# Decode attention on one core: score matmuls of four kv heads on the four 32-column groups of the PE array

## The chip, the cores and the metric

The kernel runs on one core of a Trainium2 chip. The metric is device time in microseconds; the numbers are medians of two to seven runs, which lie within about 1% of their median. A run more than 1.5% above the fastest of its kernel is called slow; the medians quoted include them, ratios and clock ranges leave them out. The profile is one execution taken by the hardware profiler; its span, from the first to the last instruction, is about 2 us shorter than the time. PE is the TensorE, PEld its weight loads, DVE the VectorE, ACT the ScalarE, POOL the GpSimd, SP the engine whose queue issues all loads here. "Granted clock" is the share of full speed that the throttle granted to the TensorE. SBUF and PSUM are on-chip memories: the loads fill SBUF, the TensorE's results land in PSUM, and to evict is to copy them from there to SBUF. A column group is 32 neighbouring columns of the TensorE's array of 128; a tile is the part of the array that one matmul uses.

## The reference

One decode step of grouped-query attention over the last 512 positions of a cache. There are 32 batches, 32 query heads, 8 kv heads, head size 128 and model size 512, all in bf16.

```python
q = (x @ wq)                                  # [32, 1, 512] @ [512, 4096] -> 32 heads of 128
k = repeat(k_cache[:, :, 2048 - 512:, :], 4)  # 8 kv heads, each for 4 query heads
v = repeat(v_cache[:, :, 2048 - 512:, :], 4)
scores = einsum("bhqd,bhkd->bhqk", q, k) * 128 ** -0.5
o = einsum("bhqk,bhkd->bhqd", softmax(scores), v)
return o.reshape(32, 1, 4096) @ wo            # [4096, 512]
```

K and V of one batch are 1 MB each, 64 MB in all; wq and wo are 4 MB each. (These MB are of 2^20 bytes; all loads together are 75.5 million bytes, and the profile counts in millions.)

## The kernel before

For each batch `b` the TensorE transposes K (32 matmuls against an identity), DVE and ACT evict K^T from PSUM to SBUF (six and two pieces of 512 columns), and eight score matmuls follow, one for each kv head. Four batches (a "quad") share one PSUM tile of 128 rows, 32 rows for each batch. Softmax, the transposes of P and the V matmuls are done a quad at a time.

```python
def load_k(b):                                  # on the SP queue; load_v is alike, with 12 buffers
    if b >= NK:                                 # NK = 4
        sp.wait_ge(pe_T3, b - NK + 1)           # buffer free: transposes of batch b - 4 done
    sp.dma_start(K_sb[:, b % NK, :, :],         # runs of KT * DH = 512 elements, 1 KB
        k_cache[b, :, SK - W:, :].rearrange("g (p kt) d -> p g (kt d)", kt=KT)).then_inc(sem_k[b % NK], 16)
# order of the loads: K0, wq, V0, K1, V1, ... K31, V31, wo

def s_matmuls(b):
    ...                                         # waits for Q of this batch and for a free PSUM tile
    for g in range(G):                          # 8 kv heads
        ...                                     # waits for the eviction of K^T of head g
        last = pe.matmul(
            S_ps[32 * j:32 * (j + 1), q % 2, :],        # j = b % 4
            lhsT=QBD[:, b % NQB, g, :],                 # 32 columns, 4 of them not zero
            rhs=KT_sb[:, b % NKT, g, :],
            start=(g == 0), stop=(g == G - 1), tile_position=(0, 32 * j))
```

All eight score matmuls of one batch use the same 32 columns of the array, so they run one after the other.

## Time and profile before

| | before |
|---|---|
| median (range), 3 runs | 229.98 us (229.43 to 230.52) |
| span of the profile | 228.2 us |
| TensorE busy | 77% |
| bytes moved by the load queue | 75.6 MB |
| mean granted clock | 0.882 |

These are lines of the page of the kernel before: the busy times of the engines, then, in 40 slices of 5.7 us, the busy share of the 16 DMA engines in tenths (9 is 90% or more), and the GB/s that they moved.

```profile
PE 176.6 (77%) x2501; PEld 124.7 (55%) x2501; DVE 90.0 (39%) x237; ACT 48.1 (21%) x93; POOL 9.4 (4%) x43
...
DMA  6999999999999999999999999999999999999950
GB/s 188 386 385 348 348 348 349 348 348 350 349 347 348 349 347 348 348 348 348 348 348 348 347 348 348 348 348 348 347 347 348 347 348 347 349 345 329 350 183 6
```

DMA is at 9 from the second slice to the 38th, and the rate is 348 GB/s in nearly all of them. It is higher, 385 and 386 GB/s, in the two slices in which wq is loaded. The rows below are of the same page's list of groups: engine, operation, output and inputs, count, then busy time in us and mean ns of one instruction, then the idle time before them and what ended most of it.

```profile
L234 PE MATMUL KT_ps<-ident,K_sb 128*128 128x128 bf16 x1024 | 74.3, 240 | 29.7 <-DMA K_sb<-in_k_cache_dram 25.6
...
L254 PE MATMUL S_ps<-KT_sb,QBD 128*32 128x512 bf16 x256 | 68.2, 414 | 2.8 <-POOL QBD L191 2.8
```

The transposes (L234) and the score matmuls (L254) are the two large items on PE. The next lines are from the list of waits (total us, times, longest): transposes that wait for K to land, and score weight loads that wait for an eviction.

```profile
PE KT_ps L234 <- DMA K_sb<-in_k_cache_dram: 25.6, 16, 2.3
...
PEld S_ps L254 <- DVE KT_sb L348: 5.9, 26, 0.3
```

The list of waits of the load queue itself names the wait for K buffers:

```profile
SPq L132 <- PE KT_ps L234: 39.8, 19, 3.5
```

One batch in the timeline (start us, duration us): the six DVE evictions, the eight score matmuls, the two ACT evictions.

```profile
141.27 2.08 DVE L348 COPY KT_sb<-KT_ps 128x512 bf16<-128x512 bf16 x6 [3.77 <-PE KT_ps L234]
...
142.44 1.90 PE L254 MATMUL S_ps<-KT_sb,QBD 128*32 128x512 bf16 x8
142.60 1.08 ACT L405 ACTIVATE KT_sb<-KT_ps 128x512 bf16<-128x512 bf16 x2 [4.77 <-PE KT_ps L234]
```

And the end of the kernel, from the same view: the first projection matmuls start at 219.61, the last eight wait 0.58 us for the last piece of wo, and the store is issued at 226.30.

```profile
219.61 3.93 PE L315 MATMUL KT_ps<-wo_sb,oT_sb 128*32 128x512 bf16 x32 [0.80 <-DVE oT_sb L370]
...
222.50 0.14 PEld L315 LDWEIGHTS KT_ps<-wo_sb,oT_sb 128*32 128x32 bf16 x8 [0.58 <-DMA wo_sb<-in_wo_dram]
...
226.30 0.35 SPq L162 DMA_DIRECT2D out_dram<-out_sb  x1
```

### The profile page before, as it was taken

Reading aid. Unit: us, or ns where it says so; the run is one execution under the profiler, and the core shown is the slowest. Engines: PE = TensorE matmul, PEld = TensorE weight load, DVE = VectorE, ACT = ScalarE, POOL = GpSimd, SP = SyncE. Lnnn points to the kernel's source line nnn. Section 1 sums busy time; section 2 is a strip of 40 time slices with the busy share of each in tenths; the row PEclk is TensorE's granted clock in tenths of the full one; section 3 lists DMA queues with packets and bytes.
Section 4 is the critical chain, followed back from the end, with each engine's and each line's share of the span. In section 5 each row is a group of like instructions: output and inputs, shape, how many; then the busy total and the mean of one; then the engine's idle time right before and its main releaser. Section 6 shows DMA issues by size and latency. Waiting matters only on the chain.

```text
span 228.2 us, 5628 instructions
## 1 busy us (share of the span) xinstructions
PE 176.6 (77%) x2501; PEld 124.7 (55%) x2501; DVE 90.0 (39%) x237; ACT 48.1 (21%) x93; POOL 9.4 (4%) x43
## 2 busy tenths in 40 slices
PE   0184968669869986995997996699669799999482
PEld 0182555447635753575564964477437656695340
DVE  0047333351535243633275243524353317644212
ACT  2000103122113211320133021321132013403203
POOL 5002000000000000000000000000000000000000
PEclk9998879999997999797699889889997859979855
DMA  6999999999999999999999999999999999999950
GB/s 188 386 385 348 348 348 349 348 348 350 349 347 348 349 347 348 348 348 348 348 348 348 347 348 348 348 348 348 347 347 348 347 348 347 349 345 329 350 183 6
DMA packets 72950, 75.90 MB, mean 333 GB/s; under 512 B 1184, under 2 KB 70880, under 8 KB 72928
## 3 DMA queue, kind: packets, MB, share of 16 engines
q1 hardware_dynamic: 72928, 75.57, 103.7%
q8 instruction: 19, 0.31, 0.6%
q14 instruction: 3, 0.02, 0.0%
HBM read 75.53 MB, written 0.03 MB: 331 GB/s over the span
## 4 chain that ended last, share of the span: by engine, by line
DMA 53%; PE 26%; SPq 16%; issue 2%; DVEq 0%; DVE 0%; ACT 0%
DMA K_sb<-in_k_cache_dram 48%; PE KT_ps L234 12%; PE S_ps L254 7%; PE QO_ps L286 6%; SPq L142 6%; DMA wo_sb<-in_wo_dram 5%; SPq L132 5%; SPq L149 4%; SPq L124 2%; PE PT_ps L266 1%; PE KT_ps L315 0%; DVEq L43 0%; DVE X_sb L389 0%; PE QO_ps L324 0%; ACT out_sb L441 0%
## 5 line engine op out<-in xcount | busy, mean ns | idle before, releaser
L234 PE MATMUL KT_ps<-ident,K_sb 128*128 128x128 bf16 x1024 | 74.3, 240 | 29.7 <-DMA K_sb<-in_k_cache_dram 25.6
L348 DVE COPY KT_sb<-KT_ps 128x512 bf16<-128x512 bf16 x192 | 68.0, 418 | 68.0 <-PE KT_ps L234 67.3
L234 PEld LDWEIGHTS KT_ps<-ident,K_sb 128*128 128x128 bf16 x1024 | 67.8, 108 | 42.1 <-DMA K_sb<-in_k_cache_dram 34.9
L254 PE MATMUL S_ps<-KT_sb,QBD 128*32 128x512 bf16 x256 | 68.2, 414 | 2.8 <-POOL QBD L191 2.8
L405 ACT ACTIVATE KT_sb<-KT_ps 128x512 bf16<-128x512 bf16 x64 | 34.7, 594 | 161.6 <-PE KT_ps L234 161.6
L254 PEld LDWEIGHTS S_ps<-KT_sb,QBD 128*32 128x32 bf16 x256 | 23.7, 102 | 34.8 <-issue 8.2
L286 PEld LDWEIGHTS QO_ps<-PT_sb,V_sb 128*128 128x128 bf16 x768 | 20.0, 97 | 3.2 <-ACT PT_sb L422 2.1
L286 PE MATMUL QO_ps<-PT_sb,V_sb 128*128 128x4 bf16 x768 | 20.7, 165 | 0.8 <-ACT PT_sb L422 0.7
L370 DVE CAST oT_sb<-QO_ps 128x128 bf16<-128x128 f32 x8 | 5.8, 719 | 38.8 <-PE QO_ps L286 38.8
L191 POOL COPY QBD<-QT_sb 128x32 bf16<-128x32 bf16 x32 | 6.3, 209 | 152.7 <-PE S_ps L254 135.8
L214 PE MATMUL QO_ps<-xT_sb,big_sb 128*128 128x32 bf16 x128 | 4.1, 185 | 8.4 <-DMA big_sb<-in_wq_dram 8.3
L336 DVE CAST QT_sb<-QO_ps 128x512 bf16<-128x512 f32 x2 | 4.8, 2393 | 13.0 <-PE QO_ps L214 13.0
L214 PEld LDWEIGHTS QO_ps<-xT_sb,big_sb 128*128 128x128 bf16 x128 | 3.8, 103 | 8.7 <-issue 6.7
L286 PEld LDWEIGHTS QO_ps<-PT_sb,big_sb 128*128 128x128 bf16 x256 | 6.5, 96 | 0.8 <-ACT PT_sb L422 0.8
L286 PE MATMUL QO_ps<-PT_sb,big_sb 128*128 128x4 bf16 x256 | 6.7, 164 | 0.0
L413 ACT ACTIVATE P_f_56<-S_ps,negmax 128x512 f32<-128x512 f32 x8 | 5.5, 687 | 4.0 <-DVE negmax L356 4.0
L354 DVE TENSOR_REDUCE maxv<-S_ps 128x1 f32<-128x512 f32 x8 | 5.5, 682 | 1.0 <-PE S_ps L254 1.0
L266 PE MATMUL PT_ps<-ident,P_bf 128*128 128x128 bf16 x32 | 3.6, 242 | 2.5 <-DVE P_bf L364 2.5
L422 ACT ACTIVATE PT_sb<-PT_ps 128x512 bf16<-128x512 bf16 x8 | 4.8, 604 | 1.2 <-PE PT_ps L266 1.2
L315 PE MATMUL KT_ps<-wo_sb,oT_sb 128*32 128x512 bf16 x32 | 3.9, 626 | 0.9 <-DVE oT_sb L370 0.8
L266 PEld LDWEIGHTS PT_ps<-ident,P_bf 128*128 128x128 bf16 x32 | 2.5, 111 | 3.0 <-DVE P_bf L364 3.0
L364 DVE TENSOR_SCALAR P_bf<-P_f_56,recip 128x512 bf16<-128x512 f32 x8 | 3.9, 486 | 0.3
(25 smaller groups left out, 14.7 us busy)
## 6 DMA issues: line engine op xcount, KB each, us to landing
K_sb<-in_k_cache_dram SPq DMA_DIRECT2D x32, 1024.0 KB, 12.1
V_sb<-in_v_cache_dram SPq DMA_DIRECT2D x24, 1024.0 KB, 12.0
big_sb<-in_v_cache_dram SPq DMA_DIRECT2D x8, 1024.0 KB, 12.0
big_sb<-in_wq_dram SPq DMA_DIRECT2D x4, 1024.0 KB, 10.8
wo_sb<-in_wo_dram SPq DMA_DIRECT2D x4, 1024.0 KB, 12.0
x_sb<-in_x_dram SPq DMA_DIRECT2D x1, 32.0 KB, 1.6
out_dram<-out_sb SPq DMA_DIRECT2D x1, 32.0 KB, 1.5
```

Source lines behind the costliest of these rows:

```text
L132: sp.dma_start(K_sb[:, b % NK, :, :], k_cache[b, :, SK - W:, :].rearrange("g (p kt) d -> p g (kt d)", kt=KT),).then_inc(sem_k[b % NK], 16)
L142: sp.dma_start(v_slot(b)[:, :, :], v_cache[b, :, SK - W:, :].rearrange("g (p kt) d -> p g (kt d)", kt=KT),).then_inc(sem_v[b % NV], 16)
L149: sp.dma_start(wo_sb[:, c * 8:(c + 1) * 8, :], wo[c * 1024:(c + 1) * 1024, :].rearrange("(h d) n -> d h n", d=P),).then_inc(sem_wo[c], 16)
L191: pool.tensor_copy(dst, src).then_inc(pool_qbd, 1)
L214: last = pe.matmul(QO_ps[:, hl * 32:(hl + 1) * 32], lhsT=wq_sb[:, kt, h * DH:(h + 1) * DH], rhs=xT_sb[:, kt, :], start=(kt == 0), stop=(kt ...
L234: last = pe.matmul(KT_ps[:, t, half * 512 + kt * 128: half * 512 + (kt + 1) * 128], lhsT=K_sb[:, b % NK, g, kt * DH:(kt + 1) * DH], rhs=id ...
L254: last = pe.matmul(S_ps[32 * j:32 * (j + 1), q % 2, :], lhsT=QBD[:, b % NQB, g, :], rhs=KT_sb[:, b % NKT, g, :], start=(g == 0), stop=(g = ...
L266: last = pe.matmul(PT_ps[:, kt * 128:(kt + 1) * 128], lhsT=P_bf[:, qq % 2, kt * 128:(kt + 1) * 128], rhs=ident[:, :], start=True, stop=Tru ...
L286: last = pe.matmul(QO_ps[:, j * 32 + 4 * g: j * 32 + 4 * g + 4], lhsT=v_slot(b)[:, g, kt * DH:(kt + 1) * DH], rhs=PT_sb[:, qq % 2, kt * 12 ...
L348: dve.tensor_copy(KT_sb[:, b % NKT, g, :], KT_ps[:, t, half * 512:(half + 1) * 512]).then_inc(dve_T, 1)
L370: dve.tensor_copy(oT_sb[:, :, 4 * qq:4 * qq + 4].rearrange("p h j -> p j h"), QO_ps[:, 0:128].rearrange("p (j h) -> p j h", h=HQ),).then_i ...
L405: act.activation(KT_sb[:, b % NKT, g, :], KT_ps[:, t, half * 512:(half + 1) * 512], ACTF.Copy).then_inc(act_T, 1)
```

## The change

The change puts head `g` on column group `g % 4`, so that matmuls which follow each other lie on different column groups and can overlap. Batches no longer own a column group; each accumulates into 4 rows of every group, and zeros in the weights keep the other rows unharmed. The weights, the number of matmuls and the loads stay as they are.

```diff
+        def prow(g, j):
+            return 32 * (g % 4) + 16 * (g // 4) + 4 * j
 ...    # the GpSimd copy of Q into QBD: same 32 elements a partition, other columns
                     last = pe.matmul(
-                        S_ps[32 * j:32 * (j + 1), q % 2, :],
+                        S_ps[32 * (g % 4):32 * (g % 4) + 32, q % 2, :],
                         lhsT=QBD[:, b % NQB, g, :],
                         rhs=KT_sb[:, b % NKT, g, :],
-                        start=(g == 0), stop=(g == G - 1), tile_position=(0, 32 * j),
+                        start=(j == 0 and g < 4), stop=(j == 3 and g >= 4), tile_position=(0, 32 * (g % 4)),
                     )
 ...    # the V matmuls read P^T at the new rows
-   rhs=PT_sb[:, qq % 2, kt * 128 + j * 32 + 4 * g: kt * 128 + j * 32 + 4 * g + 4],
+   rhs=PT_sb[:, qq % 2, kt * 128 + prow(g, j): kt * 128 + prow(g, j) + 4],
```

## The prediction

> **What bounds the kernel.** DMA. In 3 us windows the 16 DMA engines are fully busy (share 1.03 to 1.12) from 3 to 219 us, at 346 to 351 GB/s nearly everywhere (376 to 389 GB/s around the wq load, before 18 us; 333 to 339 GB/s from 201 to 210 us). The core must read 75.5 MB; at 348 GB/s that is 217 us of a 228.2 us span. The rest is the start and the tail after wo's last piece lands at 222.45 us (chain of waits): eight projection matmuls, PSUM copies, a summing matmul, a copy and the store. The TensorE is no limit: 176.6 us busy (77%), and its transposes wait 25.6 us for K to land (list of waits). The chain names PE for 26%, but those pieces gate the issue of loads that then queue: a K load lands 12.1 us after issue, at about 3 us of bandwidth each, so about four are outstanding.
>
> **What the change does.** Same 256 score matmuls, weight loads, bytes and pool copies; only the column group changes, so that neighbouring heads can overlap. Before, the eight matmuls of one batch used one column group and took about 1.90 us (timeline near 142 us). The Trainium skill, "TensorE: Matmul & The Clock Gate", Part 3 (measured speedup), gives 2.38x for three column tiles with 512 columns; not yet shown here. If all operands were ready, 1.90 us could fall to about 0.8 us. They are not: the six DVE evictions of K^T come 0.35 us apart (141.27 to 143.35) and the two of ACT end at 143.68, while the transposes end at 142.5. "TensorEngine Tiling (Array Packing)", PSUM Bottleneck, says that the PSUM copy may become the bottleneck after such a speedup; here the last matmul can't start before 143.7 and needs 0.38 us more, so it ends near 144.1 instead of 144.34. I estimate 0.2 to 0.4 us a batch, 6 to 12 us of PE time in all.
>
> **How much is critical.** Almost none. The freed PE time becomes waiting for K. At the end the chain from the last K to the projection may finish 0.3 us earlier, but the projection already waits 0.58 us for wo's last piece (list of waits), which lands when the bytes are through.
>
> **Predicted time:** 229.8 us, range 228.8 to 230.8 (before: 229.43 to 230.52). Chances: faster by over 2% 0.02, within 2% 0.96, slower 0.02.
>
> **What the profile would show if right.** DMA share full from 3 to 219 us, near 348 GB/s; wo's last piece lands within 1 us of 222.5; same tail. The score line's PE busy time falls from 68.2 us to 45 to 60 us; PE total from 176.6 to 160 to 172 us; the transposes' wait for K grows by several us. The score line's weight loads wait more for the DVE and ACT evictions. Mean granted clock between 0.82 and 0.90.
>
> **What would make it wrong.** (1) If 348 GB/s is not the ceiling of these loads but is held down by K buffers coming free late (the queue waits 39.8 us for PE), a faster PE would raise GB/s by up to a few per cent. (2) Column groups that follow each other could serialise; then the score line would not shrink, still hidden under DMA unless a batch needs over 6 us of PE time. (3) A lower clock in the tail, where it is already 0.5, could put the projection behind wo: about 0.5 us.

## The result and the profile after

| | before | after |
|---|---|---|
| median (range) | 229.83 us (229.43 to 230.52, 4 runs) | 229.61 us (229.38 to 229.70, 4 runs) |
| ratio, 95% interval | | 0.9994 (0.9972 to 1.0017) |

The time is the same. A ratio here and below is the mean time of one kernel's fast runs over that of the other's fast runs of the same rounds, so it is not quite the ratio of the medians that are quoted.

The lines of the page after that answer to those shown of before, engines and slices first:

```profile
PE 171.3 (75%) x2501; PEld 123.8 (54%) x2501; DVE 91.4 (40%) x237; ACT 48.0 (21%) x93; POOL 9.4 (4%) x43
...
DMA  5999999999999999999999999999999999999960
GB/s 175 387 386 350 348 348 349 348 348 349 349 348 350 348 350 351 348 348 350 348 350 348 350 349 348 350 348 349 349 348 348 349 348 349 349 339 334 347 208 6
```

Then the transposes and the score matmuls in its list of groups:

```profile
L242 PE MATMUL KT_ps<-ident,K_sb 128*128 128x128 bf16 x1024 | 83.5, 256 | 30.7 <-DMA K_sb<-in_k_cache_dram 27.2
...
L262 PE MATMUL S_ps<-KT_sb,QBD 128*32 128x512 bf16 x256 | 53.2, 449 | 3.6 <-POOL QBD L199 2.8
```

The loads look as before. The score matmuls fell from 68.2 to 53.2 us of busy time, 15.0 us less. TensorE as a whole fell only from 176.6 to 171.3 us, because the transposes, which the change doesn't touch, rose from 74.3 to 83.5 us. The mean granted clock of this run is 0.821, the lowest of the four (up to 0.870). Now the list of waits after:

```profile
PE KT_ps L242 <- DMA K_sb<-in_k_cache_dram: 27.2, 16, 3.7
...
PEld S_ps L262 <- ACT KT_sb L413: 16.7, 43, 0.7
...
PEld S_ps L262 <- DVE KT_sb L356: 12.4, 54, 0.2
```

The score matmuls now wait for the evictions of K^T: 16.7 us of idle weight loads for ACT and 12.4 us for DVE, against 5.9 us for DVE before. In the timeline, first the scores after of a batch with the evictions in step, then those of one whose first six heads were already evicted when the scores began, because its transposes had run slowly; the last line is the same batch in the kernel before, where all six were ready too:

```profile
142.15 1.69 PE L262 MATMUL S_ps<-KT_sb,QBD 128*32 128x512 bf16 x8
...
149.91 1.47 PE L262 MATMUL S_ps<-KT_sb,QBD 128*32 128x512 bf16 x8
...
150.25 1.90 PE L254 MATMUL S_ps<-KT_sb,QBD 128*32 128x512 bf16 x8
```

The view of the kernel after, cut short at 150.4 us so that only the first six matmuls of that second batch are merged into the line:

```profile
149.91 0.61 PE L262 MATMUL S_ps<-KT_sb,QBD 128*32 128x512 bf16 x6
```

The six ready matmuls took 0.61 us together. Before, eight in a row took 1.90 us. One lasts 0.38 us alone, so each further one then added about 0.22 us, and six would have taken about 1.5 us (worked out from these two). Column groups do overlap, for these six by about 2.4 times: by the kept trace four start within 0.01 us of each other, one on each group, and the other two follow 0.22 us later. The Trainium skill gives 2.38 times for three column tiles with 512 columns ("TensorE: Matmul & The Clock Gate", Part 3, Measured speedup); the trace agrees that tiles overlap, but six matmuls on four tiles are another arrangement, and that the two figures are so close is chance. The prediction's 0.8 us for eight ready matmuls is an estimate from that page's figure. But such a batch is the exception (7 of 32 stages took 1.47 us): in the usual one the matmuls come at the pace of the evictions, and the stage shrinks only from 1.90 to 1.69 us.

The next lines show a stretch of equal work in both traces, in windows of 3 us (busy us of PE, PEld, DVE, ACT, POOL, each with its count, then granted clock, DMA share and GB/s), before:

```profile
153.00:156.00 3.00, 3.00 (x111) 3.00 (x108) 0.53 (x1) 0.00 (x0) 0.00 (x0) 1.00 1.10 347
156.00:159.00 3.00, 3.00 (x31) 1.76 (x28) 2.10 (x7) 1.08 (x2) 0.00 (x0) 1.00 1.10 348
```

and after:

```profile
153.00:156.00 3.00, 3.00 (x86) 3.00 (x83) 0.78 (x2) 0.00 (x0) 0.00 (x0) 0.50 1.10 348
156.00:159.00 3.00, 3.00 (x29) 2.29 (x26) 2.21 (x6) 0.51 (x2) 0.00 (x0) 0.50 1.10 350
```

In this stretch the V matmuls and the next transposes ran at half clock, where they had run at full clock before. Over the whole traces, 376 transposes after and 206 before started about 0.107 us behind the one before them, and most others 0.056 us: 170 times 0.05 us is 8.5 us of the 9.2 us by which the transposes rose. The loads moved 347 to 350 GB/s in both. At the end of the kernel after:

```profile
218.98 3.92 PE L323 MATMUL KT_ps<-wo_sb,oT_sb 128*32 128x512 bf16 x32 [0.81 <-DVE oT_sb L378]
...
221.85 0.14 PEld L323 LDWEIGHTS KT_ps<-wo_sb,oT_sb 128*32 128x32 bf16 x8 [0.82 <-DMA wo_sb<-in_wo_dram]
...
225.66 0.35 SPq L165 DMA_DIRECT2D out_dram<-out_sb  x1
```

Everything is 0.63 to 0.65 us earlier than before, the wait for wo is 0.82 us, and the tail from there is as long as it was (store issued 3.8 us after that wait in both). This is within what runs of one kernel differ by.

### The profile page after: what moved, and what is told of

Its sections match the earlier page's. It is cut to its first block, busy times and chain, and to the rows that moved or that the text cites. A ratio compares the mean times of both kernels' runs of the same rounds, so it can differ in the third digit from the quotient of the medians.

```text
span 227.5 us, 5628 instructions
## 1 busy us (share of the span) xinstructions
PE 171.3 (75%) x2501; PEld 123.8 (54%) x2501; DVE 91.4 (40%) x237; ACT 48.0 (21%) x93; POOL 9.4 (4%) x43
## 4 chain that ended last, share of the span: by engine, by line
DMA 59%; PE 19%; SPq 16%; issue 3%; ACT 2%; DVEq 0%; DVE 0%; ACTq 0%
DMA K_sb<-in_k_cache_dram 54%; PE KT_ps L242 12%; PE QO_ps L294 6%; SPq L145 6%; DMA wo_sb<-in_wo_dram 5%; SPq L135 4%; SPq L152 4%; SPq L127 2%; ACT KT_sb L413 1%; ACT PT_sb L430 1%; PE KT_ps L323 0%; DVEq L43 0%; DVE X_sb L397 0%; PE QO_ps L332 0%; ACT out_sb L449 0%
## 5 line engine op out<-in xcount | busy, mean ns | idle before, releaser
L242 PE MATMUL KT_ps<-ident,K_sb 128*128 128x128 bf16 x1024 | 83.5, 256 | 30.7 <-DMA K_sb<-in_k_cache_dram 27.2
L242 PEld LDWEIGHTS KT_ps<-ident,K_sb 128*128 128x128 bf16 x1024 | 76.7, 118 | 38.9 <-DMA K_sb<-in_k_cache_dram 33.3
L356 DVE COPY KT_sb<-KT_ps 128x512 bf16<-128x512 bf16 x192 | 68.8, 418 | 64.3 <-PE KT_ps L242 63.1
L262 PE MATMUL S_ps<-KT_sb,QBD 128*32 128x512 bf16 x256 | 53.2, 449 | 3.6 <-POOL QBD L199 2.8
L262 PEld LDWEIGHTS S_ps<-KT_sb,QBD 128*32 128x32 bf16 x256 | 13.8, 95 | 36.5 <-ACT KT_sb L413 16.7
L421 ACT ACTIVATE P_f<-S_ps,negmax 128x512 f32<-128x512 f32 x8 | 5.5, 688 | 3.8 <-DVE negmax L364 3.8
L274 PE MATMUL PT_ps<-ident,P_bf 128*128 128x128 bf16 x32 | 3.1, 220 | 2.5 <-DVE P_bf L372 2.5
L368 DVE RECIPROCAL recip<-sums 128x1 f32<-128x1 f32 x8 | 1.3, 164 | 7.4 <-ACT P_f L421 7.4
L372 DVE TENSOR_SCALAR P_bf<-P_f,recip 128x512 bf16<-128x512 f32 x8 | 3.9, 486 | 0.3
```

The source lines that it names most:

```text
L242: last = pe.matmul(KT_ps[:, t, half * 512 + kt * 128: half * 512 + (kt + 1) * 128], lhsT=K_sb[:, b % NK, g, kt * DH:(kt + 1) * DH], rhs=id ...
L262: last = pe.matmul(S_ps[32 * (g % 4):32 * (g % 4) + 32, q % 2, :], lhsT=QBD[:, b % NQB, g, :], rhs=KT_sb[:, b % NKT, g, :], start=(j == 0 ...
L356: dve.tensor_copy(KT_sb[:, b % NKT, g, :], KT_ps[:, t, half * 512:(half + 1) * 512]).then_inc(dve_T, 1)
```

## The experiments

Theory A: the loads set the time; the score stage is beside the critical path, and its gain is also limited by the evictions. Rival B: K buffers that come free late hold back the loads, so a faster TensorE could speed them up. Rival C: column groups do not overlap, or overlap freely. All runs are compared with the kernel before on the same chip in the same rounds. There are three groups, each on another chip: experiments 1 to 4 (229.19 us for the kernel before), after_once_again, after_once_fill, before_2k and after_2k (229.46 us), and after_once_fill32, after_2k_warm and after_k4 (230.25 us).

### 1. dma_1k: the loads alone

All compute is removed; a buffer is loaded again once its earlier load has landed. Its output is wrong, which doesn't matter for the time.

```diff
-                    sp.wait_ge(pe_T3, b - NK + 1)
+                    sp.wait_ge(sem_k[b % NK], 16 * (b // NK))
 ...    # V alike; the programs of PE, DVE and ACT are removed, POOL writes zeros to the output
```

> Wrong result on purpose: the same loads in the same order on the same queue, a buffer is loaded again as soon as its earlier load has landed, no compute at all, zeros stored. Theory A (the 75.5 MB at 348 GB/s are the limit): last load lands near 222 us as before, 345 to 350 GB/s in the middle, total 222 to 226 us. Rival B (K buffers that come free late hold the loads back): the middle runs faster than 355 GB/s and the total is under 219 us.

Measured: 223.88 us (two runs). The rate, in 40 slices:

```profile
GB/s 173 388 387 349 348 348 348 348 348 348 348 348 348 348 348 348 348 348 348 348 348 348 348 348 348 348 348 348 348 348 348 348 348 348 348 348 348 348 348 126
```

Without any compute the loads run at the same 348 GB/s, from 20 to 200 us in both, so there no buffer, wait or engine holds them back. For this stretch rival B falls: the wait for K buffers, 39.8 us in all, did not lower the rate. The kernel before is only 5.3 us longer than its own loads. In the two profiles it issues the store 6.5 us later (226.30 against 219.81 us; its profiled run is of another round). Of these, 3.8 us are its tail after wo has landed (from 222.50 us on). The other 2.7 us come before: its loads move 339 GB/s from 200 to 219 us and 93 GB/s in the 3.5 us after that, while the loads alone move 348 until 218 us and have landed by 219.81. The wo loads are issued from 201.62 us on, alone from 198.35. What makes the loads end later beside the compute was not tested, so a late buffer is not ruled out for these 2.7 us.

### 2. dma_2k: the same bytes in longer runs

The rate during the wq load, whose runs are 2 KB, suggested that 348 GB/s belongs to the 1 KB runs of K and V. Here a partition takes 8 consecutive rows of one head, and two heads lie on alternate partitions. The compute is removed as in dma_1k.

```diff
-    sp.dma_start(K_sb[:, b % NK, :, :],
-        k_cache[b, :, SK - W:, :].rearrange("g (p kt) d -> p g (kt d)", kt=KT))
+    for h in range(2):
+        sp.dma_start(K_sb[h:P:2, b % NK, :, :].rearrange("p (t x) f -> p t (x f)", x=2),
+            k_cache[b, h:HKV:2, SK - W:, :].rearrange("t (p kt) d -> p t (kt d)", kt=2 * KT))
 ...    # V alike
```

> As dma_1k, but each contiguous run of K and V is 2 KB (8 rows of one head on a partition, two heads on alternate partitions, two DMAs of 512 KB for each former one of 1 MB). The wq load, which has 2 KB runs, moved at 384 to 389 GB/s. If the length of the run sets the rate: 375 to 390 GB/s in the middle, total 202 to 210 us. If the rate of K and V is set by something else (HBM, their addresses): 348 GB/s and 222 to 226 us as dma_1k.

Measured: 204.56 us. The rate, in 40 slices:

```profile
GB/s 141 395 386 388 387 387 386 387 386 387 387 388 386 387 386 388 387 387 388 386 388 387 387 386 387 388 387 388 386 387 386 387 387 388 386 387 385 351 348 135
```

The same bytes move at 387 GB/s, and the kernel of loads is 19.3 us shorter. The DMA engines were fully busy in both. So "fully busy" was not "at the highest rate": each engine was busy with shorter runs. (The number and size of the DMAs and the order of partitions changed too. The loads that stayed as they were speak against these: in dma_1k wq, in DMAs of 1 MB with runs of 2 KB, moves at 387 to 388 GB/s in slices 2 and 3, and in this run wo, in DMAs of 1 MB with runs of 1 KB, moves at 348 to 351 GB/s in slices 38 and 39.)

### 3 and 4. before_once and after_once: the loads taken away

To see what the change is worth where the TensorE sets the pace, both kernels load K only for the first 4 batches and V for the first 12, and reuse them. Their outputs are wrong, which doesn't matter for the times.

```diff
-            for b in range(1, B):
-                load_k(b)
+            for b in range(1, NV):
+                if b < NK:
+                    load_k(b)
                 load_v(b)
 ...
-                pe.wait_ge(sem_k[b % NK], 16 * (b // NK + 1))
+                pe.wait_ge(sem_k[b % NK], 16)          # V alike
```

> Wrong result on purpose: the kernel before with K loaded for the first 4 batches and V for the first 12 only, then reused; all compute is kept. Loads end by 75 us, after that the TensorE should set the pace: about 1.95 us of transposes, 1.9 us of scores, 0.9 us of PV and P transposes a batch. Theory: 175 to 190 us, granted clock above 0.95.

> Wrong result on purpose: the changed kernel with the same cut loads. Theory (score matmuls overlap only as far as the evictions of K^T feed them): 3 to 7% faster than before_once, about 0.2 to 0.35 us a batch. Rival (column groups do not overlap at all): within 1% of before_once. Rival (they overlap freely[...]): 15% or more faster.

Measured: 197.76 us for before_once (expected 175 to 190, a miss: the clock was 0.91 instead of over 0.95; a batch took 4.96 us from 79 to 179 us against the expected sum of 4.75, which makes 4 us of the miss, and the rest was not traced), and 192.60 us for after_once. Their ratios to the kernel before are 0.8603 (0.8568 to 0.8638) and 0.8369 (0.8314 to 0.8424); divided, 0.973, so 2.7% faster. That is just under the expected 3 to 7% and apart from both forms of rival C (within 1%, and 15% or more). The rows of transposes and scores, before_once and then after_once:

```profile
L235 PE MATMUL KT_ps<-ident,K_sb 128*128 128x128 bf16 x1024 | 71.9, 236 | 2.1 <-DMA K_sb<-in_k_cache_dram 2.1
L255 PE MATMUL S_ps<-KT_sb,QBD 128*32 128x512 bf16 x256 | 67.1, 402 | 2.8 <-POOL QBD L192 2.8
```

```profile
L243 PE MATMUL KT_ps<-ident,K_sb 128*128 128x128 bf16 x1024 | 75.0, 242 | 4.1 <-DMA K_sb<-in_k_cache_dram 4.1
...
L263 PE MATMUL S_ps<-KT_sb,QBD 128*32 128x512 bf16 x256 | 55.9, 423 | 3.7 <-POOL QBD L200 2.8
```

The waits for evictions in after_once:

```profile
PEld S_ps L263 <- DVE KT_sb L357: 18.7, 80, 0.2
...
PEld S_ps L263 <- ACT KT_sb L414: 11.1, 32, 0.7
```

The score row fell by 11.2 us and the time by 5.2 us. In this setting the evictions feed the score matmuls one by one, and 29.8 us of weight-load idle time stand for it (11.6 us in before_once). The mean granted clock was 0.909 to 0.918 in the four runs of before_once and 0.881 to 0.890 in the three fast ones of after_once, and the transposes took 3.1 us more in total. So the change works where the TensorE is the limit, but it is worth 0.16 us a batch and not the 1.3 us that a free overlap would give (an estimate: 1.90 us less the 0.61 us of the six ready matmuls, which eight on four groups, two on each, should take as well).

### 5 to 7. after_once_again, after_once_fill and after_once_fill32: where the clock went

These ask whether the short waits inside the score stage cost the granted clock. The first repeats after_once. The second puts idle matmuls of full array width into the waits, the third idle matmuls of the same 32-column form.

```diff
 ...    # in the loop over g, after the score matmul; after_once_fill:
+   if 2 <= g < G - 1:
+       for _ in range(2):
+           pe.matmul(QO_ps[:, 256:384], lhsT=ident[:, :], rhs=ident[:, :],
+                     start=True, stop=True, tile_position=(0, 0))
 ...    # after_once_fill32:
+   if 2 <= g < G - 1:
+       pe.matmul(QO_ps[32 * (g % 4):32 * (g % 4) + 32, 256:512], lhsT=ident[:, 0:32],
+                 rhs=KT_sb[:, b % NKT, g, 0:256],
+                 start=True, stop=True, tile_position=(0, 32 * (g % 4)))
```

> after_once unchanged, for a comparison on one chip: 190 to 195 us, clock 0.86 to 0.89.

> after_once with two idle 128x128 identity matmuls (to an unused part of a PSUM bank) after each of the third to seventh score matmul of a batch, where the TensorE waits 0.2 us for an eviction. Wrong result on purpose, as after_once. Theory (the waits inside the score stage cost granted clock, and this takes back part of the gain): clock back to 0.90 or more, 1 to 3 us faster than after_once_again. Rival (the lower clock has another cause, or the fillers delay the scores): clock as before, time equal or up to 5 us longer.

> after_once with one idle matmul of the same form as the score matmuls (128x32 weights, 256 columns, the column group just used) after each of the third to seventh score matmul of a batch, so that the mode of the array does not change. Wrong result on purpose, as after_once (192.6 us, clock 0.86 to 0.89). If the cost of after_once_fill was the change of mode (0.21 us each, 160 times or more), this one costs at most 3 us. If the waits in the score stage are what costs granted clock, the clock rises to 0.90 or more and the time falls by 1 to 3 us; if the clock stays below 0.89, the cause of the lower clock is something else.

Measured: 192.63, 234.18 and 192.88 us. The full-width fillers cost 41.6 us, which neither theory had expected. The timeline of PE in after_once_fill:

```profile
123.86 0.28 PE L271 MATMUL QO_ps<-ident 128*128 128x128 bf16 x2
124.07 0.39 PE L263 MATMUL S_ps<-KT_sb,QBD 128*32 128x512 bf16 x1
124.39 0.28 PE L271 MATMUL QO_ps<-ident 128*128 128x128 bf16 x2
124.61 0.39 PE L263 MATMUL S_ps<-KT_sb,QBD 128*32 128x512 bf16 x1
```

and in after_once_fill32:

```profile
125.11 0.39 PE L263 MATMUL S_ps<-KT_sb,QBD 128*32 128x512 bf16 x1
125.34 0.27 PE L270 MATMUL QO_ps<-KT_sb,ident 128*32 128x256 bf16 x1
125.45 0.39 PE L263 MATMUL S_ps<-KT_sb,QBD 128*32 128x512 bf16 x1
```

In the first, one score matmul and 256 filler columns take 0.54 us (124.07 to 124.61); in the second, the same columns take 0.34 us (125.11 to 125.45), which is the pace of the evictions. The difference goes with the change between the full array and a 32-column tile, there and back, 160 times: 0.2 us times 160 is 32 us of the 41.6; the other 10 us were not traced. The columns do not explain it: at 0.22 us for 512 columns, 768 in a row take 0.33 us. Nor do the wider weights of the fillers: 32 transposes, with weights of 128 columns, take 1.96 us, 0.06 us each. The Trainium skill says that changing the tiling mode drains the TensorE ("TensorEngine Tiling (Array Packing)", Key Properties); this pair agrees and gives the size.

On the clock the runs do not decide. The fast runs of after_once_again had 0.866 to 0.888 and those of after_once_fill, on the same chip, 0.885 to 0.899; on two other chips those of after_once_fill32 had 0.884 to 0.899 and before_once 0.909 to 0.918. The fillers recovered part of the clock at most, and no time. In every pair here the changed kernel has the lower granted clock (for the kernels before and after themselves the ranges overlap); why is left open.

### 8 and 9. before_2k and after_2k: longer runs in the whole kernel

Both kernels with the loads of dma_2k and right results. Two heads share the 128 partitions, so each K^T chunk holds both alternately.

```diff
 ...    # scores: every other column of K^T, after both evictions of the pair t
-   rhs=KT_sb[:, b % NKT, g, :],
+   rhs=KT_sb[:, b % NKT, 2 * t:2 * t + 2, h:W:2],
 ...    # P is spread over 1024 columns, zero where the row's head is not on that partition (hmask)
+   for h in range(2):
+       dve.tensor_scalar(P_bf[:, qq % 2, h:2 * W:2], P_f32[:, qq % 2, :], recip[:, qq:qq + 1],
+                         hmask[:, h:h + 1], op0=ALU.mult, op1=ALU.mult)
 ...    # 8 transposes of P instead of 4; V matmuls for two heads at once: 4 pairs x 8 chunks a batch
+   lhsT=v_slot(b)[:, 2 * t + c // 4, (c % 4) * DH:(c % 4 + 1) * DH]
```

> The kernel before (one column group a batch) with the 2 KB runs of dma_2k, results right: two heads share the 128 partitions alternately, the score matmul reads every other column of K^T and waits for both evictions of its pair, P is written twice (masked) and transposed in 8 instead of 4 pieces, and the V matmuls take two heads at once. If the loads are the limit, 204.6 us of dma_2k plus the tail of 5.5 to 6 us: 209 to 213 us, 8% faster than before. If the TensorE (198 us in before_once, plus the added work) or the strided read is in the way: 213 to 225 us.

> The changed kernel with the same 2 KB runs, results right. If the loads set the time: 209 to 212 us, within 1% of before_2k. If the TensorE has become the limit: 1 to 3% faster than before_2k, as in the pair before_once and after_once (2.6%).

Measured: before_2k 215.17 us, ratio to before 0.9369 (0.9335 to 0.9403); after_2k 214.33 us, ratio 0.9330 (0.9295 to 0.9364). Both results are correct. The load rate and the score row of after_2k:

```profile
GB/s 142 397 387 385 387 387 385 388 386 385 383 388 382 386 385 385 387 386 385 385 387 387 388 383 388 384 386 386 385 387 388 385 386 386 386 373 329 306 26 6
...
L267 PE MATMUL S_ps<-KT_sb,QBD 128*32 128x512 bf16 x256 | 43.3, 429 | 11.7 <-DVE KT_sb L370 4.6
```

The loads run at 382 to 388 GB/s in slices 3 to 35 and end near 204 us; the rest is a longer tail, because the last batches' chain through transposes, softmax, V and projection is now longer than the load of wo that used to hide it: in the trace the projection waits 0.81 us for oT and no longer for wo. So the time is 214 us and not the 210 us of dma_2k plus the old difference of 5.3 us. The two differ by 0.4% with overlapping intervals, so the column groups are worth nothing clear here either. Their clocks were 0.896 to 0.917 (before_2k) and 0.829 to 0.860 (after_2k).

### 10. after_2k_warm: the tail at full clock

```diff
+   keep_busy(40)                     # idle 128x128 identity matmuls
     pt_transposes(NQUAD - 1)
+   keep_busy(16)
     pv_matmuls(NQUAD - 1)
```

> after_2k, results right, with idle 128x128 matmuls while the TensorE waits for the last softmax (40) and for the last eviction of P (16). In after_2k the clock is 0.5 there and the last V stage takes 3.6 us, the projection 3.2 us. If they keep the clock at 1.0: 1 to 2 us faster than after_2k (214.3 us). If the fillers overrun the wait: same or slower.

Measured: 213.06 us, ratio to before 0.9257 (0.9220 to 0.9293), correct: the best version, 7.4% faster than before.

From the start of the last P transposes to the issue of the store, after_2k took 12.29 us (198.00 to 210.29) and after_2k_warm 11.79 us (197.63 to 209.42): the P transposes and their eviction became 0.43 us shorter, the V stage 0.22 us (3.58 to 3.36), while the projection, which the fillers no longer preceded, was no faster. So about 0.5 us of the gain is located, less than the 1 to 2 us that were expected. By the two ratios it is 0.8%, but the two kernels ran on different chips in different rounds, and the intervals (up to 0.9293, from 0.9295) all but touch.

### 11. after_k4: K in 4 KB runs

K only, four heads interleaved over the partitions, V as in after_2k. The score matmul then reads every fourth column and waits for all evictions of its four heads.

```diff
-   rhs=KT_sb[:, b % NKT, 2 * t:2 * t + 2, h:W:2],
+   rhs=KT_sb[:, b % NKT, 4 * t:4 * t + 4, h:W:4],
 ...    # 4 DMAs of 256 KB with runs of 4 KB; P is written in the matching order
```

> after_2k with K in 4 KB runs (16 rows of a head on a partition, four heads interleaved over the partitions, four DMAs of 256 KB), V still in 2 KB runs, results right; the four heads of a group become ready together, so four column groups really start at once. From 1 KB runs at 348 GB/s and 2 KB at 387 I estimate a fixed cost per run that gives about 410 GB/s for 4 KB, so the K stream saves 4 to 5 us. If the loads still set the pace: 209 to 211 us. If the TensorE's own chain at the end and its pace are the limit: 213 to 215 us, as after_2k.

Measured: 222.71 us, 8 us slower than after_2k, correct. Neither number was met. The rate and the score row (the profiled run is a slow one, so only the kind of the lines counts):

```profile
GB/s 159 329 393 394 397 398 398 397 401 393 396 397 395 397 397 399 398 397 396 399 397 398 399 396 398 396 396 335 354 407 393 378 358 363 349 257 0 0 3 6
...
L266 PE MATMUL S_ps<-KT_sb,QBD 128*32 128x512 bf16 x256 | 51.6, 609 | 25.9 <-ACT KT_sb L429 13.5
```

The loads did rise to 393 to 401 GB/s (slices 3 to 27; 4 KB for K, 2 KB for V), then fell. By the traces the TensorE did not follow: a score matmul lasts 609 ns instead of 429, and the array stood idle for 13.5 us waiting for ACT, since whole groups of evictions must end first. Four tiles at once are not enough to make matmuls longer: in the kernel after (at 149.91 us) and in after_2k (at 101.74 us) four also start within 0.01 us of each other, and each lasts 0.39 and 0.40 us there, reading every column and every second one. That leaves the reads at every fourth column, which no run tests alone; the profile models the ends of matmuls.

## Why the prediction was right

The prediction (229.8 us, 228.8 to 230.8) held: 229.61 us. Point by point:

- *DMA bounds the kernel, almost nothing of the change is critical.* Right, and shown: the loads alone take 223.88 us, all but 5.3 us of the time. The rate stayed the same, and the end of the wo load moved by only 0.65 us. (About 2.7 us of the profile lie in loads that end later beside the compute, experiment 1; the prediction did not see this.)
- *348 GB/s as the bound.* Right for these loads, but it is the rate of 1 KB runs and not a ceiling of the core: dma_2k moves the same bytes at 387 GB/s. The prediction quoted the 376 to 389 GB/s of the wq load and did not follow it up. Its rival, K buffers that come free late, does not explain the 348 GB/s, by dma_1k.
- *The score line falls to 45 to 60 us, PE to 160 to 172 us.* Right: 53.2 and 171.3 us. The estimate of 6 to 12 us for the score stage was too small; it fell by 15.0 us. It was made from a batch of the usual kind at full clock, and for those it was right: 26 of the 32 score stages became 0.27 us shorter on average, 6.9 us together (1.90 to 1.69 us, or to 1.47 us where six heads were ready). It left out the other six, which ran at a clock of 0.50 to 0.86 before: they took 2.19 to 3.60 us, and 1.69 to 2.16 us after, also at a lowered clock, which saves 7.3 us. (The last 0.8 us are gaps inside the stages.) At a clock of 0.50 the matmuls had followed each other at 0.43 us, slower than the evictions at 0.35 us, so there overlap gained more.
- *The evictions become the limit of the stage.* Right: 16.7 us of waits for ACT and 12.4 us for DVE. The skill's warning in "TensorEngine Tiling (Array Packing)", PSUM Bottleneck, fits these numbers.
- *The freed time becomes waiting for K, several us.* Wrong: 25.6 us became 27.2 us. Of the 15.0 us, 9.2 us went to the transposes, which ran at half clock more often in the profiled run, the one with the lowest clock of its four. The prediction allowed for a lower clock (0.82 to 0.90; measured 0.821 to 0.870 in four runs) but did not say that it would take the freed time.

## What to carry to other kernels

A faster stage on an engine that waits for loads gave nothing here (ratio 0.9994); measure the loads alone before tuning the compute beside them. A busy DMA share says only that the engines are occupied: compare the GB/s of different loads in one trace, and where longer contiguous runs move faster, lay the data out for them (here 6 to 7%). Column groups help only as far as their inputs are ready together, and switching between the full array and a column tile has a price (0.2 us there and back), so group the matmuls of one form.

## What the Trainium skill lacked or had wrong

- "DMA: Bandwidth & Descriptors", Specifications, names 512 B as the minimum transfer for line rate. Here 1 KB runs moved at 348 GB/s and 2 KB runs at 387 GB/s, with all 16 engines busy and no compute (223.88 against 204.56 us). This concerns that row, which gives one threshold, and not what the page says elsewhere of the cost of small descriptors.
- The same section gives about 358 GB/s as the limit of HBM for each core (another section of the page says that a core alone measures more). One core alone held 385 to 388 GB/s in 35 of 40 slices here (dma_2k), as that other section has it; the row by itself misleads for a core alone.
- "TensorEngine Tiling (Array Packing)", Key Properties, says that a change of mode drains the array, but gives no size. Here a change from a 32-column tile to the full array and back cost 0.2 us (0.54 against 0.34 us for the same columns), and 160 of them, by that figure, 32 of 41.6 us.
- "TensorE: Matmul & The Clock Gate" does not say what column groups do to the granted clock. Here it was lower with them: 0.857 to 0.909 in the 21 runs of the kernel before that ran beside the experiments, 0.821 to 0.870 in the 4 of the kernel after; 0.909 to 0.918 against 0.881 to 0.890 (fast runs) in the pair without loads after the start; 0.896 to 0.917 against 0.829 to 0.860 in the pair with 2 KB runs. The cause is open.
